# A gated mix of cached attention and a feed-forward block, one decode step: the query projection on TensorE as a register loop instead of 128 written-out products

## The chip, the core and the metric

The kernel runs on one core of one Trainium2 chip. The metric is the device time of that core in microseconds, one launch of the whole program. Three runs of the kernel before gave 2520.60, 2520.71 and 2520.96 us; the median is 2520.71 us.

## What is computed

One token `x` of 512 numbers passes through two branches, which a scalar gate mixes. Branch A is attention over a cache of 65,536 keys and values for each of 32 heads of 128 dimensions; branch B is a feed-forward block with a hidden size of 1,792.

```python
g = sigmoid((x * gate_w).sum(-1, keepdims=True))
q = (x @ wq).reshape(B, Sq, 32, 128).transpose(0, 2, 1, 3)      # x: 1 x 512, wq: 512 x 4096
p = softmax(einsum("bhqd,bhkd->bhqk", q, k_cache) * 128**-0.5)  # k_cache: 32 heads x 65536 x 128, bf16
o = einsum("bhqk,bhkd->bhqd", p, v_cache)
a = o.transpose(0, 2, 1, 3).reshape(B, Sq, 4096) @ wo
b = (silu(x @ w_gate) * (x @ w_up)) @ w_down                    # 512 x 1792, 512 x 1792, 1792 x 512
return g * a + (1 - g) * b
```

The keys and values of one head are 16.8 MB each, so the whole launch has to read 1,088 MB from device memory.

## The kernel before

The program gives each engine one list of instructions and orders them by semaphores that are written out by hand; there is no scheduler. In the names below `sp` is SyncE, which issues nearly all transfers, `pe` TensorE, `dve` VectorE, `act` ScalarE and `pool` GpSimd. An engine takes its own list strictly in order.

**The transfers (L213 to L247).** SP issues, in order, the query weights `wq` (4.2 MB, into the memory region `V0`), `wg`, `wu` and `wd` of the feed-forward block (1.8 MB each), and the first half of the keys of head 0 in two pieces of 4.2 MB, signalled by `ka0` and `ka`. These six need no wait. At L221 SP waits for `s_q`, which TensorE sends when the query projection is done, because the second half of head 0's keys (8.4 MB, `load("k", 0, 1)`, signalled by `kz`) goes into the region `V0`, over `wq`. From head 1 on, a loop (L223 to L235) issues four loads of 8.4 MB for each head: first half of its keys, first half of the values of the head before, second half of the keys, second half of those values. Each load waits until its buffer is free: the count of key transposes done (`ktdone`), or of value products done (`pvdone`). For head 1, the first load waits for 8 transposes (`NP`), and the load of the values behind it for 13 transposes and for `s_b`, the end of the feed-forward block. All of these loads travel on one queue.

**TensorE's start (L433 to L482).** TensorE turns `x` into a column with four products, then computes the query projection: for each of 32 heads, four products of a 128 x 128 block of `wq` (the stationary side) with a 128 x 1 column of `x`, added up in one column of the PSUM bank `psM`. The last one sends `s_q`. Behind it in TensorE's list are four products that spread the query over rows (L449, which wait for the copy L374 on VectorE), the broadcast of the gate (L453), the 112 products of the feed-forward block's first layer (`mlp_up`, L471), its 14 products with `wd` (L479), and then the loop over the heads (L491).

**VectorE's start (L373 to L388).** VectorE copies the query (L374), lays it out in `qd` (L377), waits for ScalarE's `s_sig` and `s_gc`, finishes the feed-forward block's hidden vector `guT` (L382 to L386), and only then begins to transpose the keys of head 0 (`transposes(0)` and `transposes(1)`, L334): eight transposes for each half, the first four wait for `ka0`, the next four for `ka`. There are two buffers for transposed keys, so transpose number i waits until TensorE has finished the scores (L459) of number i - 2.

**ScalarE's start (L285 to L290).** ScalarE copies the query of head 0 (L286, behind VectorE's `qd`), then the gate column (L288, which sends `s_gc`; `mlp_up` waits for it), then takes the exponential of L290.

**The loop over the heads** is a register loop on TensorE (`nc.tensor.Fori(0, H)`, L491) and on VectorE (L390): the loop index sits in a register, and waits for counts such as `n + (NP * z + c + 1)` (L496) are computed from it by register instructions. In the kernel before, no product and no transpose has an address that depends on a register; only the counts waited for do.

**The end (L514 to L559).** The last head's values are multiplied in eight pieces (L520) as they land, then the output projection follows.

Of the kernel before, what the change touches and what calls it, by code (L numbers as in the profile page):

```python
# [20 lines left out]
def bass_gated_mix__mha_block_cached__swiglu_ffn__decode_kernel(  # L21
# [11 lines left out]
    out: bass.AP,  # L33
):
    _, H, S, Dh = A_k_cache.shape
    D = A_wq.shape[0]
    F = B_w_gate.shape[1]
    Dc = D // P
# [24 lines left out]
    with ExitStack() as ctx:  # L63
        def sb(name, shape, dt):
            return ctx.enter_context(nc.sbuf_tensor(name, shape, dt))

        def psum(name, shape, dt):
            return ctx.enter_context(nc.psum_tensor(name, shape, dt))
# [7 lines left out]
        psM = psum("psM", [P, 512], F32)  # L76
# [18 lines left out]
        xTb = sb("xTb", [P, 16], BF16)  # L95
# [11 lines left out]
        def at(kb, n):  # L107
            return mem[:, kb * KB:kb * KB + n]
# [76 lines left out]
        wq_ap = at(WQ, Dc * H * Dh).rearrange("p (c n) -> p c n", c=Dc)  # L185
# [246 lines left out]
        def _(pe):  # L432
# [3 lines left out]
            for c in range(Dc):  # L436
                last = nc.tensor.matmul(psM[:, c:c + 1], xv[:, c, :], ones[0:1, 0:1], start=True, stop=True)
            last.then_inc(s_xT, 1)
            pe.wait_ge(s_xTb, 1)
            pe.wait_ge(d["wq"], 16)  # L440
            for h in range(H):
                for c in range(Dc):
                    last = nc.tensor.matmul(psM[:, 128 + h:129 + h], wq_ap[:, c, h * Dh:(h + 1) * Dh],  # L443
                                            xTb[:, c:c + 1], start=(c == 0), stop=(c == Dc - 1))
            last.then_inc(s_q, 1)
            pe.wait_ge(s_qTb, 1)
            pe.wait_ge(s_sel, 1)
            for je in range(4):
                last = nc.tensor.matmul(psQ[:, je, 0:H], sel[:, je, :], qTb[:], start=True, stop=True)  # L449
# [28 lines left out]
            for j in range(FC):  # L478
                last = nc.tensor.matmul(psY[0:1, :], guT[:, j:j + 1], wd_ap[:, j, :],  # L479
                                        start=(j == 0), stop=False)  # L480
# [10 lines left out]
            with nc.tensor.Fori(0, H) as i:  # L491
                n = i * (2 * NP)
                pe.wait_ge(s_qc, i + 1)
                for z in range(2):
# [3 lines left out]
                    with nc.tensor.If(i > 0):  # L498
# [5 lines left out]
                        for part, rows in enumerate(v_order[z]):  # L504
                            for m, r in enumerate(rows):
                                last = nc.tensor.matmul(psO[0:4, :], pb[:, 256 * z + r:256 * z + r + 4],  # L506
                                                        vt[:, r * Dh:(r + 4) * Dh],
                                                        start=(z == 0 and part == 0 and m == 0),
                                                        stop=(z == 1 and part == 1 and m == len(rows) - 1))
# [4 lines left out]
            def piece(n):  # L514
# [3 lines left out]
                for r in range(nr):  # L518
# [12 lines left out]
                             start=True, stop=True).then_inc(s_R, 1)  # L531
            pe.wait_ge(s_oR, 1)
            pe.wait_ge(d["wo"], 16)
            for j in range(31):
                last = nc.tensor.matmul(psY[0:1, :], oR[:, j:j + 1], wo_ap[:, j, :], start=False, stop=(j == 30))  # L535
# [4 lines left out]
            for c in range(4):  # L540
                nc.tensor.matmul(psZ[0:4, 0:128], hot[0:1, c, :], yrow[0:1, 128 * c:128 * c + 128],
                                 start=(c == 0), stop=False)
# [9 lines left out]
            for e in range(2):  # L552
# [3 lines left out]
                for c in range(4):  # L556
                    last = nc.tensor.matmul(psZ[0:4, 0:128], w4[:, e, c, :], w2_ap[:, e, c, :], start=False,  # L557
                                            stop=(e == 1 and c == 3))
# [29 lines left out]
```

## Time and profile before

| what | value |
|---|---|
| median of 3 runs | 2520.71 us |
| the profiled execution, whole | 2520.63 us |
| its span, first to last instruction | 2518.8 us |
| moved from device memory | 1087.77 MB, 432 GB/s over the span |
| TensorE busy, share of the span | 1584.4 us, 63% |
| VectorE busy, share of the span | 1397.4 us, 55% |
| ScalarE and GpSimd busy | 65.6 us and 26.9 us |
| mean granted TensorE clock | 0.711 |
| instructions in the profile | 46,364 |

The profiled execution is 1.8 us longer than its span: what lies before the first and behind the last instruction. The rows of the profile give a group of instructions by line, engine and operation, its output and inputs, the count, the busy time, the mean time of one, and the idle time of the engine before them with what ended it. In the timeline the first two columns are the start and the length in us, counted from the start of the span. `SPq` and `ACTq` are transfers issued by SyncE and ScalarE; `PEld` is TensorE's load of the stationary side, which overlaps its products; `PEldq` are instructions of TensorE's sequencer (register work, branches, semaphores), which aren't counted as busy.

### The profile page before, as it was taken

What the parts mean: (1) busy time and instruction counts of PE and PEld (TensorE: products, weight loads), DVE (VectorE), ACT (ScalarE), POOL (GpSimd) and SP (SyncE); (2) the same over time, 40 slices, a digit from 0 to 9 for tenths busy, and PEclk for the clock granted to TensorE, in tenths of its full rate; (3) what the DMA queues carried; (4) which work ended last, traced back from release to release, by engine and by line L of the source; (5) the groups of instructions that cost most, each with busy time, mean ns of one, the idle gap of its engine ahead of it and who ended that gap; (6) DMA issues with size and microseconds to landing.
All of it is one profiled execution on the core that took longest, in us unless ns stands there. A gap on an engine that the chain in (4) does not pass through costs nothing.

```text
span 2518.8 us, 46364 instructions
## 1 busy us (share of the span) xinstructions
PE 1584.4 (63%) x21432; PEld 889.3 (35%) x21432; DVE 1397.4 (55%) x1630; ACT 65.6 (3%) x195; POOL 26.9 (1%) x83
## 2 busy tenths in 40 slices
PE   3556756666666576565675665666657656567567
PEld 3333333333333333333333333333333333333334
DVE  3764565554655645646446555465464564644653
ACT  0000000000000000000000000000000000000000
POOL 0000000000000000000000000000000000000000
PEclk8667767677676676676776766767667667677676
DMA  9999999999999999999999999999999999999999
GB/s 418 433 435 433 433 433 433 434 433 434 433 433 433 433 433 433 433 433 434 433 434 433 433 433 433 431 435 434 433 437 434 434 433 435 434 434 433 433 431 391
DMA packets 20476, 1088.00 MB, mean 432 GB/s; under 512 B 2282, under 2 KB 2668, under 8 KB 2924
## 3 DMA queue, kind: packets, MB, share of 16 engines
q1 hardware_dynamic: 20448, 1087.78, 99.9%
q8 instruction: 11, 0.18, 0.0%
q14 instruction: 5, 0.04, 0.0%
q10 hardware_dynamic: 12, 0.00, 0.0%
HBM read 1087.77 MB, written 0.00 MB: 432 GB/s over the span
## 4 chain that ended last, share of the span: by engine, by line
DMA 73%; DVE 14%; issue 11%; PE 1%; DVEq 0%; SPq 0%; ACT 0%
DMA mem<-in_A_k_cache_dram 71%; DVE kt L409 7%; DVE kt L402 6%; DMA mem<-in_A_wo_dram 1%; PE psO L506 1%; DMA mem<-in_A_v_cache_dram 1%; DVE kt L334 0%; DVE pb L343 0%; DVEq L407 0%; SPq L211 0%; DVEq L400 0%; PE psZ L557 0%; PE psS L459 0%; SPq L219 0%; ACT fin L311 0%
## 5 line engine op out<-in xcount | busy, mean ns | idle before, releaser
L459 PE MATMUL psS<-qcur,kt 128*128 128x4 bf16 x16384 | 515.8, 167 | 888.6 <-DVE kt L402 553.6
L506 PE MATMUL psO<-mem,pb 128*4 128x512 bf16 x3968 | 998.8, 417 | 17.9 <-DMA mem<-in_A_v_cache_dram 17.9
L402 DVE STREAM_TRANSPOSE kt<-mem 128x2048 uint32<-128x2048 uint32 x248 | 551.2, 2280 | 579.2 <-DMA mem<-in_A_k_cache_dram 578.2
L459 PEld LDWEIGHTS psS<-qcur,kt 128*128 128x128 bf16 x16384 | 473.2, 104 | 957.3 <-DVE kt L402 586.8
L409 DVE STREAM_TRANSPOSE kt<-mem 128x2048 uint32<-128x2048 uint32 x248 | 547.5, 2274 | 407.8 <-DMA mem<-in_A_k_cache_dram 407.8
L506 PEld LDWEIGHTS psO<-mem,pb 128*4 128x4 bf16 x3968 | 354.1, 91 | 619.1 <-issue 184.7
L343 DVE COPY pb<-pa 32x64 bf16<-32x64 bf16 x1024 | 233.3, 228 | 25.4 <-PE psO L506 10.6
L334 DVE STREAM_TRANSPOSE kt<-mem 128x2048 uint32<-128x2048 uint32 x16 | 35.4, 2276 | 17.1 <-DMA mem<-in_A_k_cache_dram 17.1
L348 DVE TENSOR_REDUCE sm<-psS 128x1 f32<-128x512 f32 x32 | 22.1, 692 | 35.4 <-PE psS L459 35.4
L298 ACT ACTIVATE oTn<-psT,gcol 128x1 bf16<-128x1 f32 x31 | 8.2, 263 | 1113.2 <-PE psT L486 1113.2
L275 POOL PARTITION_ALL_REDUCE sm<-sm x32 | 11.2, 351 | 2392.6 <-DVE sm L348 2392.6
L486 PEld LDWEIGHTS psT<-unit,orow 4*128 4x128 f32 x256 | 30.8, 186 | 14.9 <-issue 13.5
L486 PE MATMUL psT<-unit,orow 4*128 4x1 f32 x256 | 33.5, 248 | 0.8 <-ACT orow L296 0.8
L296 ACT ACTIVATE orow<-psO,sm 4x512 f32<-4x512 f32 x31 | 21.0, 677 | 446.2 <-issue 446.2
L302 ACT ACTIVATE sm<-sm 128x1 f32<-128x1 f32 x32 | 6.5, 203 | 831.4 <-POOL sm L275 831.4
L304 ACT ACTIVATE pa<-psS,sm 128x512 bf16<-128x512 f32 x32 | 22.0, 687 | 1.0
L520 PE MATMUL psW<-pb,mem 128*128 128x1 bf16 x512 | 14.4, 165 | 4.8 <-DMA mem<-in_A_v_cache_dram 3.4
L520 PEld LDWEIGHTS psW<-pb,mem 128*128 128x128 bf16 x512 | 14.0, 102 | 6.0 <-issue 4.5
L277 POOL PARTITION_ALL_REDUCE sm<-sm x32 | 12.3, 383 | 36.4 <-ACT pa L304 36.4
L443 PE MATMUL psM<-xTb,mem 128*128 128x1 bf16 x128 | 3.6, 165 | 11.4 <-DMA mem<-in_A_wq_dram 11.4
L471 PE MATMUL psM<-xTb,mem 128*128 128x1 bf16 x112 | 6.9, 198 | 4.7 <-DMA mem<-in_B_w_up_dram 4.7
L535 PE MATMUL psY<-mem,oR 128*1 128x512 bf16 x31 | 9.5, 480 | 0.3 <-DVE oR L423 0.3
(63 smaller groups left out, 57.1 us busy)
## 6 DMA issues: line engine op xcount, KB each, us to landing
mem<-in_A_v_cache_dram SPq DMA_DIRECT2D x3, 4096.0 KB, 27.6
mem<-in_A_k_cache_dram SPq DMA_DIRECT2D x2, 4096.0 KB, 38.8
mem<-in_A_wq_dram SPq DMA_DIRECT2D x1, 4096.0 KB, 12.9
mem<-in_A_wo_dram SPq DMA_DIRECT2D x1, 3968.0 KB, 32.7
mem<-in_A_v_cache_dram SPq DMA_DIRECT2D x1, 2048.0 KB, 32.0
mem<-in_B_w_gate_dram SPq DMA_DIRECT2D x1, 1792.0 KB, 16.7
mem<-in_B_w_up_dram SPq DMA_DIRECT2D x1, 1792.0 KB, 21.3
mem<-in_B_w_down_dram SPq DMA_DIRECT2D x1, 1792.0 KB, 25.1
```

The lines of the kernel that those rows point to most:

```text
L277: nc.gpsimd.partition_all_reduce(Lt, rsum, P, RADD).then_inc(s_L, 1)
L296: nc.scalar.mul(orow[0:4, :], psO[0:4, :], Li[0:4, :]).then_inc(s_or, 1)
L304: nc.scalar.activation(pa[:], psS[:], ACT.Exp, bias=nbias, scale=SCALE, accum_out=rsum).then_inc(expdone, 1)
L334: nc.vector.transpose(kt[:, i % 2, :].rearrange("p (j r t) -> p r j t", j=2, t=32), src.rearrange("p (r j t) -> p r j t", j=2, t=32)).then ...
L343: last = nc.vector.tensor_copy(dst, sr)
L348: nc.vector.reduce_max(mxs, psS[:], AX_X).then_inc(s_mx, 1)
L402: nc.vector.transpose(kt[:, c % 2, :].rearrange("p (j r t) -> p r j t", j=2, t=32), src.rearrange("p (r j t) -> p r j t", j=2, t=32)).then ...
L409: nc.vector.transpose(kt[:, c % 2, :].rearrange("p (j r t) -> p r j t", j=2, t=32), src.rearrange("p (r j t) -> p r j t", j=2, t=32)).then ...
L459: last = nc.tensor.matmul(psS[:, col + 4 * r:col + 4 * r + 4], ktb[c % 2][:, je // 2, r, :, je % 2], qcur[:, je, :], start=(je == 0), stop ...
L486: last = nc.tensor.matmul(psT[:, 0:1], orow[0:4, i * Dh:(i + 1) * Dh], unit[0:4, i:i + 1], start=(i == 0), stop=(i == 3))
L506: last = nc.tensor.matmul(psO[0:4, :], pb[:, 256 * z + r:256 * z + r + 4], vt[:, r * Dh:(r + 4) * Dh], start=(z == 0 and part == 0 and m = ...
L520: last = nc.tensor.matmul(psW[:, 0:1], vt[:, r * Dh:(r + 1) * Dh], pb[:, col:col + 1], start=(col == 0), stop=(col == R - 1))
```

## The change

The loop over heads in the query projection, which was unrolled when the program was built, becomes a loop on the chip over the first 31 heads. The head's number is in a register of TensorE, and both the column of `psM` that a product writes and the block of `wq` that it loads are addressed by values computed from that register. The four products of the last head stand behind the loop, with fixed addresses, and the last of them sends `s_q` as before. The products, their order, their data and all waits are the same.

```diff
             pe.wait_ge(s_xTb, 1)
             pe.wait_ge(d["wq"], 16)
-            for h in range(H):
+            with nc.tensor.Fori(0, H - 1) as h:
                 for c in range(Dc):
-                    last = nc.tensor.matmul(psM[:, 128 + h:129 + h], wq_ap[:, c, h * Dh:(h + 1) * Dh],
-                                            xTb[:, c:c + 1], start=(c == 0), stop=(c == Dc - 1))
+                    nc.tensor.matmul(psM[:, bass.ds(h + 128, 1)], wq_ap[:, c, bass.ds(h * Dh, Dh)],
+                                     xTb[:, c:c + 1], start=(c == 0), stop=(c == Dc - 1))
+            for c in range(Dc):
+                last = nc.tensor.matmul(psM[:, 127 + H:128 + H], wq_ap[:, c, (H - 1) * Dh:H * Dh],
+                                        xTb[:, c:c + 1], start=(c == 0), stop=(c == Dc - 1))
             last.then_inc(s_q, 1)
```

`nc.tensor.Fori(0, H - 1)` runs its body 31 times with h from 0 to 30; `bass.ds(start, size)` is a slice whose start is a register value; `H` is 32, `Dc` is 4 and `Dh` is 128.

## The prediction

> **What bounds the kernel now.** I read the page's slices and queues first, then the timeline of the first 60 us, the chain of waits, SyncE's own waits, and last the source view of the loop that TensorE already has. The page:
>
> ```profile
> DMA  9999999999999999999999999999999999999999
> q1 hardware_dynamic: 20448, 1087.78, 99.9%
> DMA 73%; DVE 14%; issue 11%; PE 1%; DVEq 0%; SPq 0%; ACT 0%
> L443 PE MATMUL psM<-xTb,mem 128*128 128x1 bf16 x128 | 3.6, 165 | 11.4 <-DMA mem<-in_A_wq_dram 11.4
> ```
>
> Transfers are busy in every slice, and one queue holds 99.9% of 16 engines' span: the time is bytes over 433 GB/s, plus whatever moment the queue is empty. The changed products (L443) take 3.6 us in all, 27.8 ns for each (3.56 / 128). So the edit can matter only by making a transfer start late. The stretch in which it could:
>
> ```profile
> 13.73 3.56 PE L443 MATMUL psM<-xTb,mem 128*128 128x1 bf16 x128 [11.35 <-DMA mem<-in_A_wq_dram]
> 17.32 0.33 SPq L207 DMA_DIRECT2D mem<-in_A_k_cache_dram  x1
> 19.84 0.15 ACT L288 COPY gcol<-psM 128x2 f32<-128x2 f32 x1
> 23.03 6.87 PE L471 MATMUL psM<-xTb,mem 128*128 128x1 bf16 x112 [4.66 <-DMA mem<-in_B_w_up_dram]
> 31.05 0.23 DVE L386 TENSOR_SCALAR guT<-hbuf,gcol 128x14 bf16<-128x14 f32 x1
> 31.43 4.66 PE L479 MATMUL psY<-mem,guT 128*1 128x512 bf16 x14 [1.53 <-DVE guT L386]
> 36.93 8.89 DVE L334 STREAM_TRANSPOSE kt<-mem 128x2048 uint32<-128x2048 uint32 x4 [5.65 <-DMA mem<-in_A_k_cache_dram]
> 55.57 0.33 SPq L207 DMA_DIRECT2D mem<-in_A_k_cache_dram  x1
> ```
>
> Call the end of the L443 products Q; it is 17.29. At 17.32 SyncE issues the second half of head 0's keys. The next issue, head 1's keys, comes at 55.57, when eight transposes are done. The chain and SyncE's waits say the same:
>
> ```profile
> 46.65 8.90 DVE kt L334 x4
> 55.57 29.92 DMA mem<-in_A_k_cache_dram
> ...
> SPq L207 <- DVE kt L334: 59.2, 2, 37.9
> SPq L207 <- PE psM L443: 13.7, 1, 13.7
> ```
>
> That transfer lands at 85.49, 29.9 us after its issue, though 8.39 MB need only 19.4 us at 433 GB/s. The rest is queue ahead of it: this is the cover behind which Q can move.
>
> **How far Q can move for nothing.** From Q the timeline gives fixed steps. The gate column (L288) ends at 19.99, Q + 2.7; `mlp_up` waits for it and, at present, longer for `wu` (23.03). It takes 6.87. L386 ends 1.38 behind it (31.28 against 29.90). So VectorE is free for the first transpose at Q + 11.0, and TensorE, whose L479 starts 1.53 behind `mlp_up` and takes 4.66, is free for scores at Q + 15.8. Transposes follow each other by 2.19 us and the last takes 2.28 (four in 8.9). The third needs the scores of the first (1.0 us), so it starts at about Q + 17, and the eighth ends at Q + 17 + 5 x 2.19 + 2.28 = Q + 30.3. SyncE issues head 1's keys there, or at 55.57 if that is later. A transfer into an empty queue takes 3.2 us besides its bytes: `wq`, the first, has 12.9 us to landing in the page's issues and 9.7 us of bytes (4.19 MB at 433 GB/s). Head 1's keys then land at Q + 30.3 + 19.4 + 3.2 = Q + 52.9 against 85.5. **The loss is Q - 32.6, and nothing below that.** Q has 15.3 us to give. The earlier gap, where head 0's second half itself starts late (the queue's first six loads have all landed at 46.62), lies inside this loss for every Q above 32.6, as the same chain sets the later issue. Behind it nothing recovers: transfers are the bound in all slices that follow, so lost queue time stays in the total. The load behind, head 0's values, needs 13 transposes, 5 x 2.19 = 11 us after the eighth, and head 1's keys are in transit for 22.6 us then: hidden.
>
> **What the loop costs.** Removed: 31 x 4 products at 27.8 ns, 3.45 us. Added: 31 rounds. No wait is added, but `s_q`, and everything named above, stands behind the loop in TensorE's list: SyncE's load at L222, VectorE's copy L374, ScalarE's two copies. The trace of before has no product with a register address. It does have TensorE's register loop:
>
> ```profile
> L491 PEldq FUSED_REGOPS  x32: 41/41/46, 31.7 to 2401.6; - x32
> L491 PEldq ALU_OP  x32: 36/36/36, 84.7 to 2479.2; - x32
> L491 PEldq COMPARE_BRANCH  x32: 67/209/219, 84.8 to 2479.3; - x32
> L496 PEldq ALU_OP  x480: 32/32/42, 39.7 to 2463.6; - x160
> ```
>
> Durations alone mislead here; starts count. Narrow windows of 0.02 us over the loop's entry put MOVE, FUSED_REGOPS and L496's FUSED_REGOPS at 31.64, 31.72 and 31.84: one sequencer instruction per **0.10 us**, of which 0.033 to 0.046 is its own duration and about 0.065 lies around it. The first closing shows ALU_OP at 84.70, COMPARE_BRANCH at 84.80 and the next round's first instruction at 85.06: **0.36 us** to close a round. L496 also shows that a computed value costs a separate ALU_OP (15 of 16 waits in a round have one) and that what stands together is fused.
>
> Per round then:
> - closing, 0.36;
> - addresses: one fused group for the first `wq` block and the column, and one ALU_OP for each of the other three blocks, 4 x 0.10 = 0.40 (low end one group, 0.10; high end nine separate instructions, 0.90);
> - four products, each a weight load with a register address and a product with a register address: eight instructions. Low end 4 x 0.028 = 0.11, as if they went like the fixed ones. High end 8 x 0.10 = 0.80, each handled like a register instruction. They are nearest to an instruction that the sequencer must read registers for but does not execute itself, between 0.065 and 0.10; I take 0.08, together 0.64.
>
> Sum 1.40 us a round; low 0.57, high 2.06. Four fixed products behind take 0.11. Start 13.73, so Q = 13.73 + 31 x 1.40 + 0.11 = **57.2**; low 31.5, high 77.7. The loss is 57.2 - 32.6 = **24.6 us** (low none, high 45). Span 2518.8 + 24.6 = 2543.4; with the 1.8 us outside the span, 2545.2, and the median of before is 0.1 above its profiled run: 2545.3 us.
>
> [...]
>
> **Shorter code.** Some 248 fixed instructions fewer shift where TensorE's instruction blocks begin (11 instruction packets on q8). The tail shows one unexplained stop, 1.30 us of "issue" ahead of L520 at 2512.30, hidden since the last piece of values lands at 2515.2 anyway. Moved behind that landing it would cost up to 1.3, moved away it gains nothing. I take nothing, and 1.3 for the range.
>
> **Rivals.**
> - *The cover holds (not slower).* If a round stays at or under (32.6 - 13.84) / 31 = 0.605 us, Q stays under 32.6 and the time is 2520.7. For it: 15.3 us of cover are real. Against it: closing and one register group are 0.46 already, which leaves 0.145 for eight instructions and all other addresses. Up to 0.77 us the loss is still under 5 us.
> - *Products at their old pace.* Register work as above, products at 27.8 ns: 0.36 + 0.40 + 0.11 = 0.87, Q = 40.8, loss 8.2, 2529. For it: products are queued and the array is far from busy. [...]
> - *Each product waits for the one before.* Load 104 ns and product 165 ns no longer overlap: 4 x 0.27 more, 2.48 a round, Q = 90.7, loss 58, 2579. Nothing in the trace shows such a drain around register work; L506 and L459 run on between ALU_OPs.
> - *Fetching code at each jump back.* A stop like the 1.30 us one at every closing: 31 x 1.3 = 40 more, loss 65, 2586. Against it: 32 closings of the long loop over the heads have a maximum of 219 ns. [...]
> - *No loop is built,* the products stay written out: 2520.7. The 32 branches of L491 say such a loop is real.
>
> **Chances.** Forecast (2531 to 2562) 0.65; old pace 0.16; cover holds 0.09; waits between products 0.06; code fetch 0.03; no loop 0.01. I call 0.2%, 5 us, what a measurement of this kernel tells from no change. Slower is 0.65 + 0.16 + 0.06 + 0.03 = 0.90, plus 0.01 of the cover case's upper edge; same 0.07; faster 0.02, for a luckier tail or start. The range takes in the old pace and the forecast with its tail, and leaves out about 0.19: 2525 to 2562.
>
> **What would show it.** Right: some 31 COMPARE_BRANCH in the new loop's line about 1.4 us apart; SyncE's issue of head 0's second half at about 57; the first transposes at about 68 and head 1's keys issued near 88; the first two slices of GB/s well under 433, the others as before; span near 2543. Each step has its own row: rounds (Q), Q + 11.0 to the first transpose, Q + 30.3 to the issue. The forecast is wrong if Q is under 33, if the queue stays fed though Q is late, or if the loop over the heads itself becomes slower.

## The result, and the profile after

The changed kernel takes 2534.57 us (median of 6 runs, 2533.72 to 2536.57) against 2520.84 us (6 runs, 2520.60 to 2521.01): the ratio is 1.0056, with a 95% interval of 1.0046 to 1.0067. It is slower by 13.7 us. The profiled execution took 2534.45 us with a span of 2532.6 us, 13.8 us more than the span of before.

The page of the changed kernel, its transfers by slice (GB/s in 40 slices of 63 us) and the main queue, and last the GB/s row of the kernel before:

```profile
DMA  9899999999999999999999999999999999999999
GB/s 402 354 438 431 433 433 431 439 435 432 434 431 432 439 433 433 434 431 434 436 435 433 433 431 437 434 433 436 431 432 437 433 434 435 431 433 435 435 433 388
q1 hardware_dynamic: 20448, 1087.78, 99.4%
...
GB/s 418 433 435 433 433 433 433 434 433 434 433 433 433 433 433 433 433 433 434 433 434 433 433 433 433 431 435 434 433 437 434 434 433 435 434 434 433 433 431 391
```

The bytes are the same and every slice from the third to the last but one moves 431 to 439 GB/s (431 to 437 before); the last has 388 (391 before). Only the first two fall: 402 and 354 where the kernel before had 418 and 433. The 16 and 79 GB/s that are missing there, over 63 us each, are 6.0 MB, or some 14 us at 433 GB/s. So the whole loss lies in the first 126 us. The timeline there (start, length, engine and line, count):

```profile
14.15 0.58 PE L443 MATMUL psM<-xTb,mem 128*128 128x1 bf16 x4 [11.66 <-DMA mem<-in_A_wq_dram]
15.21 0.56 PE L443 MATMUL psM<-xTb,mem 128*128 128x1 bf16 x4 [0.48 <-issue]
...
44.56 0.59 PE L443 MATMUL psM<-xTb,mem 128*128 128x1 bf16 x4 [0.44 <-issue]
45.23 0.26 PE L446 MATMUL psM<-xTb,mem 128*128 128x1 bf16 x4
45.51 31.18 SPq L207 DMA_DIRECT2D mem<-in_A_k_cache_dram  x2
48.24 6.88 PE L474 MATMUL psM<-xTb,mem 128*128 128x1 bf16 x112 [1.67 <-ACT gcol L288]
56.41 4.50 DVE L334 STREAM_TRANSPOSE kt<-mem 128x2048 uint32<-128x2048 uint32 x2
56.65 5.48 PE L482 MATMUL psY<-mem,guT 128*1 128x512 bf16 x14 [1.53 <-DVE guT L386]
63.06 30.82 DVE L334 STREAM_TRANSPOSE kt<-mem 128x2048 uint32<-128x2048 uint32 x14 [2.15 <-PE psS L462]
```

Each row of four products is one round of the loop; they start 1.01 us apart. The query products end at Q = 45.49, where they ended at 17.29 before. The SPq row merges two issues of 0.33 us: the second half of head 0's keys at 45.51, and head 1's keys, which end the row, at 76.36. VectorE's third transpose at 63.06 waited 2.15 us for scores, which stand behind the `wd` products (L482) in TensorE's list. The end of the chain of waits in this stretch:

```profile
62.13 0.90 PE psS L462 x32
63.04 0.02 issue
63.06 3.45 DVE kt L334 x2
66.51 0.98 issue
67.49 8.86 DVE kt L334 x4
76.35 0.02 issue
76.36 23.28 DMA mem<-in_A_k_cache_dram
```

Head 1's keys need 23.28 us from issue to landing, where they needed 29.92 before: there is no queue ahead of them any more. The gap itself shows in windows of 2 us (engine busy times with counts, then granted clock, busy share of the transfers, GB/s):

```profile
64.00:66.00 2.00, 0.57 (x21) 0.57 (x22) 2.00 (x2) 0.00 (x0) 0.00 (x0) 0.69 1.21 524
66.00:68.00 2.00, 0.82 (x31) 0.74 (x29) 2.00 (x2) 0.00 (x0) 0.00 (x0) 0.50 0.03 8
68.00:70.00 2.00, 0.82 (x31) 0.74 (x28) 2.00 (x2) 0.00 (x0) 0.00 (x0) 0.50 0.00 0
70.00:72.00 2.00, 0.83 (x32) 0.74 (x28) 2.00 (x2) 0.00 (x0) 0.00 (x0) 0.50 0.00 0
72.00:74.00 2.00, 1.02 (x32) 0.93 (x32) 2.00 (x1) 0.00 (x0) 0.00 (x0) 0.50 0.03 8
74.00:76.00 2.00, 1.02 (x32) 0.93 (x32) 2.00 (x2) 0.00 (x0) 0.00 (x0) 0.50 0.00 0
76.00:78.00 2.00, 1.02 (x32) 0.93 (x32) 2.00 (x2) 0.00 (x0) 0.00 (x0) 0.50 1.47 492
...
44.00:46.00 2.00, 1.21 (x15) 0.83 (x14) 0.19 (x1) 0.00 (x0) 0.00 (x0) 1.00 0.16 66
46.00:48.00 2.00, 0.57 (x5) 0.48 (x2) 1.75 (x4) 0.08 (x1) 0.00 (x0) 1.00 1.51 524
```

For 10 us, from 66 to 76, almost nothing moves (8 GB/s at most), while VectorE (third figure) transposes without a break: the transfers wait for transposes that are late. The last two rows show a smaller gap of some 1.7 us around 45, before head 0's second half is issued. The source view of the loop has what a round is made of (duration in ns min/median/max, first and last start):

```profile
L441 PEldq FUSED_REGOPS  x31: 78/78/88, 13.9 to 44.3; - x31
L441 PEldq ALU_OP  x31: 36/36/42, 14.6 to 45.0; - x31
L441 PEldq COMPARE_BRANCH  x31: 76/208/248, 14.7 to 45.1; - x31
L443 PEldq FUSED_REGOPS  x124: 42/46/51, 14.1 to 44.9; - x124
L443 PE MATMUL psM<-xTb,mem x124: 181/184/184, 14.1 to 45.0; 128*128 128x1 bf16 x124
```

One group of register operations opens a round, one stands ahead of each of the four products, and an addition and a branch close it. The branch came 30 times between 14.7 and 45.1, every 1.013 us.

### The profile page after: what moved, and what is told of

Same layout as the page of the kernel before. It is cut to its first block, busy times and chain, and to the rows that moved or that the text cites. A ratio compares the mean times of both kernels' runs of the same rounds, so it can differ in the third digit from the quotient of the medians.

```text
span 2532.6 us, 46582 instructions
## 1 busy us (share of the span) xinstructions
PE 1603.5 (63%) x21432; PEld 900.4 (36%) x21432; DVE 1397.5 (55%) x1630; ACT 65.6 (3%) x195; POOL 27.0 (1%) x83
## 4 chain that ended last, share of the span: by engine, by line
DMA 72%; DVE 14%; issue 12%; PE 2%; DVEq 0%; SPq 0%; ACT 0%
DMA mem<-in_A_k_cache_dram 69%; DVE kt L409 7%; DVE kt L402 6%; DMA mem<-in_A_v_cache_dram 2%; PE psO L509 1%; PE psM L443 1%; DMA mem<-in_A_wq_dram 1%; DVE kt L334 0%; PE psM L474 0%; PE psY L482 0%; DVE pb L343 0%; DVEq L407 0%; PE psS L462 0%; DVE qd L377 0%; SPq L244 0%
## 5 line engine op out<-in xcount | busy, mean ns | idle before, releaser
L443 PE MATMUL psM<-xTb,mem 128*128 128x1 bf16 x124 | 17.6, 183 | 25.0 <-issue 13.4
L443 PEld LDWEIGHTS psM<-xTb,mem 128*128 x124 | 12.9, 104 | 29.8 <-issue 27.5
L523 PE MATMUL psW<-pb,mem 128*128 128x1 bf16 x512 | 14.7, 165 | 4.7 <-DMA mem<-in_A_v_cache_dram 3.1
## 6 DMA issues: line engine op xcount, KB each, us to landing
mem<-in_A_wq_dram SPq DMA_DIRECT2D x1, 4096.0 KB, 12.9
mem<-in_B_w_gate_dram SPq DMA_DIRECT2D x1, 1792.0 KB, 16.8
```

The source lines that it names most:

```text
L443: nc.tensor.matmul(psM[:, bass.ds(h + 128, 1)], wq_ap[:, c, bass.ds(h * Dh, Dh)], xTb[:, c:c + 1], start=(c == 0), stop=(c == Dc - 1))
L523: last = nc.tensor.matmul(psW[:, 0:1], vt[:, r * Dh:(r + 1) * Dh], pb[:, col:col + 1], start=(col == 0), stop=(col == R - 1))
```

## The experiments

The theory under test: the loop costs time only through Q; Q delays the eighth transpose, this the issue of head 1's keys (called A), and the queue runs dry. The rivals: the load held back at L221 is what costs; the loop itself disturbs something lasting; or every round costs from the first one on. "Loss" in this part is against the kernel before of the same chip, by medians where there are several runs.

**A loop over some of the heads.** The bound of the loop is changed and the remaining heads are written out behind it, here for 15; 22 and 8 likewise.

```diff
-            with nc.tensor.Fori(0, H - 1) as h:
+            with nc.tensor.Fori(0, 15) as h:
                 ...
-            for c in range(Dc):
-                last = nc.tensor.matmul(psM[:, 127 + H:128 + H], ...
+            for h in range(15, H):
+                for c in range(Dc):
+                    last = nc.tensor.matmul(psM[:, 128 + h:129 + h], wq_ap[:, c, h * Dh:(h + 1) * Dh], ...
```

> The loop covers the first 15 heads only, the other 17 are written out. Theory (late start): the loss is Q - 32, Q being the end of the query products; with rounds of 1.01 us Q = 14.2 + 15 x 1.01 + 17 x 0.111 = 31.2, so no loss: 2520.5 to 2521.5. Rival (the register loop disturbs something lasting, such as where code blocks begin or how TensorE runs on): the loss of 13.7 us stays, or half of it: 2527 to 2535.

> The loop covers 22 heads, the other ten are written out. Late start: Q = 14.2 + 22 x 1.01 + 10 x 0.111 = 37.5, loss Q - 32 = 5.5, or 6 with the 0.9 by which the full loop lay above its sum: 2526 to 2527. Loss in proportion to the rounds from the first one on: 22/31 x 13.7 = 9.7: 2530.5. Loss independent of the rounds: 2534.5.

Measured: with 15 heads Q was 31.1 and A 61.1; 2521.30 us against 2520.70, ratio 1.0006 (0.9996 to 1.0016): no loss that can be told; the interval ends at a loss of 4.0, where a price per round would be 6.6. With 22 heads Q was 37.5 and A 68.4; 2526.11 us, ratio 1.0022 (1.0013 to 1.0032), a loss of 5.4. The first fifteen rounds show no cost and the next seven cost what the late start says, so a price per round from the first one on and a lasting disturbance by the loop are out. The runs with 15 heads scattered, though, from 2520.51 to 2524.45, while the kernel before kept within 2520.37 to 2521.14; that led to a loop over 8 heads.

> The loop covers the first 8 heads, 24 are written out: Q = 14.2 + 8 x 1.01 + 24 x 0.028 x 4 = 25.0, and head 1's keys are issued at Q + 30 = 55 to 56, some 6 us ahead of the edge at 61 to 62 on which the loop of 15 heads sits. If that loop's runs of up to 3.8 us more are small delays between Q and that issue which only count at the edge: 2520.4 to 2521.2 with a spread like that of before. If a register loop brings the scatter by itself: again single runs 2 to 4 us above the lowest.

Measured: Q 24.8, A 55.9; 2520.86 us against 2520.66, ratio 1.000 (0.9991 to 1.001), runs from 2520.59 to 2522.20, the kernel before from 2520.40 to 2522.37. Away from the edge the scatter is that of the kernel before.

**Only the load late, only TensorE late.** In the kernel before, with the products written out, first the load, then TensorE:

```diff
             sp.wait_ge(s_q, 1)
+            sp.wait_ge(d["ka"], 16)
             load("k", 0, 1)
```

> Products written out as before; only the load of the second half of head 0's keys is held until the first half has landed (46.6), so it is issued about 1 us later than with the loop, while TensorE and VectorE are on time. If the loss comes by way of the eighth transpose and the load behind it: the keys land at 46.65 + 22.6 = 69.2 in place of 66.2, the next load is issued at 55.55 in time, loss about 3: 2523 to 2524.5. If it comes by way of this late load itself: loss about 14: 2534 to 2536.

```diff
             pe.wait_ge(d["wq"], 16)
+            for m in range(120):
+                nc.tensor.matmul(psZ[:], wq_ap[:, 0, 0:128], wq_ap[:, 0, 0:512], start=True, stop=True)
```

> Products written out as before, but 120 wide products into an unused bank go ahead of them (their result is used by nothing), so that Q is late without any loop: at 0.22 us each, 0.43 while the clock is low, Q = 14 + 28 to 35 + 3.6 = 45 to 52. Late start: loss is Q - 32 + about 0.5 with the Q that the trace shows, 13 to 21: 2534 to 2542. If it is the loop as such: no loss, 2521.

Measured: the late load alone gave 2524.29 us, ratio 1.0014 (1.0004 to 1.0024), a loss of 3.6. It was issued at 46.88, later than the loop's 45.51, and cost a quarter of the loop's loss. Its chain of waits:

```profile
46.82 8.90 DVE kt L335 x4
55.72 0.02 issue
55.74 33.60 DMA mem<-in_A_k_cache_dram
```

Head 1's keys are issued at 55.74, in time, and find 3.7 us more queue ahead of them (33.60 against 29.92): the gap ahead of the late load, no more. TensorE kept busy instead put Q at 45.3 with no loop in the program; A was 75.35 and the time 2533.84 us, ratio 1.0053 (1.0036 to 1.0070), a loss of 13.1. Lateness alone makes the loss, whatever makes it late.

**The load not held back.** The full loop, but the part of head 0's second half that does not lie over `wq` is issued ahead of the wait.

```diff
+            kz0 = kv_dram(A_k_cache, 0)[1]
+            sp.dma_start(at(V0 + 32, half), kz0[:, half:2 * half]).then_inc(d["kz1"], 16)
             sp.wait_ge(s_q, 1)
-            load("k", 0, 1)
+            sp.dma_start(at(V0, half), kz0[:, 0:half]).then_inc(d["kz"], 16)
```

> The full loop, but the second half of head 0's keys is two loads: the 4.2 MB that do not lie over wq are issued without waiting for the query products, the rest behind them; head 0's second transposes wait for both. The queue then holds 9.7 us more ahead of Q. If the eighth transpose sets the loss: it comes at 76.4 as with the loop alone and nothing is won, 2533.5 to 2536 (at most 2 us less). If the load held back at L221 sets it: all 13.7 come back, 2521.

Measured: 2535.39 us, ratio 1.0056 (1.0039 to 1.0073): nothing came back, though the queue no longer ran empty while SyncE waited at L221: from 44 to 46 us it moved 492 GB/s where the loop alone moved 66. SyncE's issues, two windows of this kernel, and the same two of the loop alone:

```profile
45.46 0.33 SPq L224 DMA_DIRECT2D mem<-in_A_k_cache_dram  x1
76.73 0.33 SPq L207 DMA_DIRECT2D mem<-in_A_k_cache_dram  x1
...
30.00:60.00 30.00, 19.88 (x191) 14.96 (x192) 6.49 (x12) 0.45 (x3) 0.00 (x0) 1.00 0.99 427
60.00:90.00 30.00, 15.45 (x426) 12.62 (x425) 27.43 (x14) 0.00 (x0) 0.00 (x0) 0.59 0.56 232
...
30.00:60.00 30.00, 19.82 (x190) 14.91 (x191) 6.43 (x12) 0.45 (x3) 0.00 (x0) 1.00 0.97 409
60.00:90.00 30.00, 15.45 (x439) 12.97 (x438) 27.85 (x14) 0.00 (x0) 0.00 (x0) 0.58 0.61 251
```

From 30 to 60 us it moves 427 GB/s where the loop alone moves 409; from 60 to 90 it moves 232 where the loop alone moves 251. What the early load won, the wait for the eighth transpose took back, as A is the same (76.7 against 76.4).

**What a round is made of.** Three kernels keep the 128 products written out, as before, and put a loop of 31 rounds ahead of them: with fixed addresses, with only the column from the register, with only the block of `wq` from the register. The product in the loop's body, beside that of the changed kernel:

```diff
-                    nc.tensor.matmul(psM[:, bass.ds(h + 128, 1)], wq_ap[:, c, bass.ds(h * Dh, Dh)],
+                    nc.tensor.matmul(psM[:, 200:201], wq_ap[:, c, 0:Dh],                    # fixed
+                    nc.tensor.matmul(psM[:, bass.ds(h + 128, 1)], wq_ap[:, c, 0:Dh],        # column
+                    nc.tensor.matmul(psM[:, 200:201], wq_ap[:, c, bass.ds(h * Dh, Dh)],     # block
```

> 31 rounds of four products with fixed addresses into an unused column (head 0's blocks each time), then all 128 products written out as before. It measures a round without register addresses. If the register work is the price: closing 0.36 + 4 x 0.028 = 0.47 us a round, Q = 14.0 + 31 x 0.47 + 3.6 = 32.2, loss 0 to 0.5: 2521. If the loop's closing is the price: 0.9 to 1.0 us a round and Q near 48.

> As e6, with the column written taken from the register and the block of wq fixed (head 0's). If the column is computed once a round: 0.47 + 0.10 to 0.15 = 0.6 us a round, Q = 36, loss 4: 2525. If each product has its own register instruction for it: 0.47 + 4 x 0.10 + 0.1 = 0.97, Q = 48, loss 16: 2537.

> As e6, with the block of wq taken from the register and a fixed unused column. If the block's address is what each product's register instruction computes: 0.9 to 1.0 us a round, Q = 46 to 48, loss 14 to 16: 2535 to 2537. If the two addresses need separate work and the column has the larger share: 0.6 to 0.7 us, Q = 37 to 39: 2526 to 2528.

The branches of the fixed, the column and the block kernel, and the register work of the last two, from their source views (the fixed kernel has no FUSED_REGOPS row):

```profile
L441 PEldq COMPARE_BRANCH  x31: 76/208/240, 14.4 to 26.0; - x31
```
```profile
L441 PEldq COMPARE_BRANCH  x31: 76/208/243, 14.4 to 29.5; - x31
L441 PEldq FUSED_REGOPS  x31: 53/53/59, 14.1 to 29.3; - x31
```
```profile
L441 PEldq COMPARE_BRANCH  x31: 76/208/243, 14.7 to 42.0; - x31
L441 PEldq FUSED_REGOPS  x31: 68/68/74, 14.1 to 41.3; - x31
L443 PEldq FUSED_REGOPS  x93: 46/46/46, 14.2 to 41.7; - x93
```

First and last start, over 30 rounds, give 0.39, 0.50 and 0.91 us a round; the changed kernel has 1.01.

| loop | register groups in a round, besides the closing | us a round | above fixed, per group |
|---|---|---|---|
| fixed | 0 | 0.39 | |
| column | 1 | 0.50 | 0.12 |
| block | 4 | 0.91 | 0.13 |
| changed kernel | 5 | 1.01 | 0.125 |

A round is the closing and its products, 0.39, and 0.12 to 0.13 for each group of register operations. The column kernel bounds what a register address can cost a product: its four products and their one group add 0.117 us a round together, so the products have at most 0.03 each. In the block kernel the four loads and their four groups add 0.52; by the column's price of a group 0.06 is left for the four loads, which is what remains of an address on a load. The times, of one run each, 2521.66, 2523.44 and 2533.74 us, rise with Q (29.7, 33.2 and 45.7). All three came earlier than expected: 29.7 for 32.2, 33.2 for 36, and 45.7 for 46 to 48.

**Four heads a round.**

```diff
+            with nc.tensor.Fori(0, H - 4, 4) as h:
+                for k in range(4):
+                    for c in range(Dc):
+                        nc.tensor.matmul(psM[:, bass.ds(h + (128 + k), 1)], wq_ap[:, c, bass.ds(h * Dh + k * Dh, Dh)], ...
```

> The loop takes four heads a round, seven rounds, and the last four heads are written out. Closing 0.36 and group 0.10 once per four heads, 16 products at 0.13: 2.54 us a round; Q = 14.1 + 7 x 2.54 + 16 x 0.028 = 32.3. Late start: loss Q - 32 = 0 to 1: 2520.6 to 2522. If every product's register work grows with the heads in a round, or the loss belongs to any register loop: 2525 to 2535.

Measured: a round takes 2.65 us, Q is 33.3 and A 63.7; 2522.11 us against 2520.78, ratio 1.0008 (0.9999 to 1.0018), runs from 2521.50 to 2526.51. Opening and closing a round once for four heads brings Q down by 12 us; the register group ahead of every one of the 16 products stays. It sits just past the edge.

All kernels together, spans of the profiled executions against 2518.8, with the length of the 14 `wd` products, which lie between Q and A in TensorE's list:

| kernel | Q | `wd` products | A | span, more than before |
|---|---|---|---|---|
| before | 17.3 | 4.66 | 55.6 | |
| only the load late | 17.4 | 4.82 | 55.7 | 3.8 |
| loop of 8 heads | 24.8 | 5.67 | 55.9 | 0.8 |
| fixed addresses | 29.7 | 5.97 | 61.1 | 1.1 |
| loop of 15 heads | 31.1 | 4.59 | 61.1 | -0.1 |
| column from the register | 33.2 | 5.29 | 63.9 | 2.8 |
| four heads a round | 33.3 | 5.07 | 63.7 | 2.1 |
| loop of 22 heads | 37.5 | 5.50 | 68.4 | 5.8 |
| TensorE late, no loop | 45.3 | 4.64 | 75.4 | 12.6 |
| block from the register | 45.7 | 4.47 | 75.6 | 13.1 |
| the change | 45.5 | 5.48 | 76.4 | 13.8 |
| the change, load split | 45.4 | 5.91 | 76.7 | 15.8 |

In the ten kernels below the first two rows, A is Q + 25.4 + the length of the `wd` products, in each within 0.02 us when Q and A are read to two places. So in these traces nothing else between Q and A varies, loop or no loop. From an A of 68 on, the loss is A - 62.6 within 0.2 us, and 1.7 more for the split load, whose profiled execution was the slowest of its four. With A between 55.9 and 61.1 it is 1.1 us at most, and the two kernels at 63.7 and 63.9 lie 1.0 and 1.5 us above the line; single runs scatter by as much. None of these is faster than the kernel before, and none was expected to be: its transfers are busy in every slice already.

## Why the prediction was right, and where it was not

**The path.** It held step by step. SyncE's load followed Q at once (45.51); VectorE's first transpose started at Q + 10.9, foretold as Q + 11.0; head 1's keys were issued at Q + 30.9, foretold as Q + 30.3. That the earlier gap "lies inside this loss" is what the split load showed: it filled that gap and won nothing. The kernel with TensorE late and no loop shows the same path with the loop taken out.

**The edge.** "The loss is Q - 32.6, and nothing below that": for Q = 45.5 this gives 12.9, measured 13.8 by span. Ahead of the issue lies 0.6 of it: the `wd` products took 5.48 us where 4.66 was taken over from before, 0.8 more, of which 0.2 was covered by rounding Q + 16.8 up to "about Q + 17". The landing adds 0.7 (23.28 for 22.6), and what follows it gives 0.4 back.

**The round: the mis-sized term.** Forecast 1.40 us, measured 1.01: Q came at 45.5 and not at 57.2, 11.7 us earlier, and with the 0.9 of the edge this is why 2545 was forecast and 2534.6 came. Of its three terms:
- products, 0.64 for eight instructions at 0.08 each: measured, next to nothing above the pace of fixed products (at most 0.03 for a product, about 0.01 for a load). This is the step that failed. The price taken was the author's estimate, set between 0.065 and 0.10, the figures of register instructions in the trace of before; no run shows it for a product or a load. The low end, 0.11 for all eight, was nearest.
- addresses, 0.40 for four instructions at 0.10: measured 0.62, five groups at 0.125. The first product has a group of its own, which was assumed to be the same as the group that opens the round.
- closing, 0.36: with four products 0.39 together, where 0.47 was the sum; the products of a round still run while it closes (in the first round of the changed kernel to 14.73, with the closing addition starting at 14.6).

The rival "products at their old pace" had the right rule for products, but with four groups of registers a round it came to 0.87 and 2529. With five groups at 0.125, and 0.39 for closing and products, it is 1.01, which by the prediction's own edge gives 2533. The forecast and this rival were thus one mechanism with one unknown price, and the result lies between their two times. The product rule that held is the rival's; that the time still fell among the forecast's, from 2531 on, is luck, because the addresses were priced 0.22 too low while the products were priced over 0.5 too high.

**The other rivals.** The cover does hold up to its edge: 15 rounds show no cost. Products do not wait for each other (four of them take 0.58 us with four register groups among them), and the jump back shows no stop for code (208 ns median, 248 at most). The page of the profile has 10 instruction packets where there were 11. The stop of "issue" among the last value products, 1.30 us before, is 1.47 us in the changed kernel and absent with 15 heads, 22 heads or four heads a round. That it follows where code blocks begin was argued, not tested; it stayed hidden behind the last pieces' landing in the changed kernel, where TensorE still waited 0.41 us for them.

**Open.** The runs of the changed kernel spread over 2.9 us, those with 15 heads over 3.9 and those with four heads a round over 5.0, while the kernel before spread over 0.4 to 2.0 beside the various kernels. With 8 heads, away from the edge, the spread was 1.6 against 2.0 before. That fits a delay between Q and A which counts only from the edge on, and the traces name one: the `wd` products, 4.47 to 5.97 us long. That is 1.5 us, and each kernel has one trace, so whether it makes the whole scatter is not shown; the late load alone, with A in time, spread over 2.3.

## What to carry to other kernels

When one queue is full all the time, an engine's list has a budget rather than a price (here 15 rounds cost nothing that can be told, and 22 cost 5.4 us): follow the late instruction to the next transfer that waits for it, here through eight transposes, and count how much is queued ahead of that transfer. The nearest wait in the code need not be the one that decides, as filling the gap behind it won nothing. For a register loop on TensorE like this one, an estimate from these runs is 0.12 to 0.13 us for each of the sequencer's groups of register operations, and 0.39 for the closing with four products at their usual pace. Five separate addresses in a round took five groups here, and the twenty of four heads a round took seventeen.

## What was not expected of the hardware

A product whose weight block and column come from registers costs TensorE next to nothing that the rounds can show (at most 0.03 us for the product and about 0.01 for its load). Its record is 184 ns long where the fixed one has 165 (165 with only the column from the register, 184 with only the block), but rounds grow almost only by the register groups.

The same 14 `wd` products took 4.66 us before and 5.48 us behind the loop, and 4.47 to 5.97 us in the twelve traces. The source view of the changed kernel:

```profile
L482 PE MATMUL psY<-mem,guT x14: 379/634/634, 56.7 to 61.8; 128*1 128x512 bf16 x14
```

Part of the way through, the starts change from 0.43 us apart to 0.21 us apart, and single records from 634 ns to 379 ns: in the changed kernel 4.7 us behind the first start, in the kernel before 3.0, in the twelve traces 2.6 to 5.7. The granted clock is what changes there. In each trace a clock record of 1.00 begins while the product runs at which the pace changes. In the kernel with TensorE kept busy the view has the clock at 0.50 from 56.5 to 59.4 us and at 1.00 from 59.5 to 61.1, with products of 631 ns in the first stretch and 379 ns from 59.7 on. The other traces have no clock record ahead of that point, and the view prints 1.00 where there is none; so the 1.00 from 44 to 48 us in the windows above, and in all windows that early, does not say that the clock was at full speed. The twelve switches spread over 3.0 us. In the kernel before and in the changed one the lengths of the clock records, 3.41 to 71.68 us, are multiples of 3.41 us, but for the last record of each. What sets the moment of the switch is not shown. The longer `wd` products behind the loop thus come from where that switch falls and not from the loop: the kernel with only the block from the register, whose Q is as late, had the shortest of all, 4.47 us.
